# Gate first, then up in place, and a second Strassen level for one product of a gated feed-forward block

## The chip, the cores and the metric

The kernel runs on one core of one Trainium2 chip. The metric is the device time of one launch in microseconds (us); the profile's span, from the first to the last instruction, is 1.7 to 1.8 us shorter. A core has a matmul engine (TensorE, PE in the profile; its weight loads are a row of their own, PEld), VectorE (DVE), ScalarE (ACT), GpSimd (POOL) and a queue for transfers (SP). The kernel's matmuls read their operands from SBUF and write to PSUM, which the kernel uses as 8 banks of 512 fp32 columns. All runs told of here are with a granted TensorE clock of 0.999 or 1.000.

## The reference

A block of linear attention is followed by a gated feed-forward block (FFN), bf16, 2048 tokens, width 1024, hidden width F = 3584. Only the second half matters here:

```
h    = x + attention(layernorm(x))
n    = layernorm(h)
gate = n @ W_gate;  up = n @ W_up        # 1024 x 3584 each
gate = gate * (gate > 0)                 # ReLU
out  = h + (gate * up) @ W_down          # 3584 x 1024
```

## The kernel before

The tokens are taken in two passes of 1024. In each pass the gate and up products come first, then the down product. Products are done with Strassen's method (Winograd's form): 7 products of halved blocks stand in for 8, at the price of sums of the blocks before and of partial results after. The down product mostly uses two levels of it, gate and up one level.

One call of `strassen_pair` is a *unit*: two tiles of 128 columns of F, for gate (`w` = 0) and up (`w` = 1). `prod` is 4 matmuls of 512 columns into one PSUM bank. `S` are sums of token blocks, made once a pass; `T` are sums of weight blocks, made on VectorE one unit ahead (`fillin`). ScalarE forks a partial result to a second bank (`fk1`, `fk2`) so that two outputs can share it.

```python
BA, BE, BB, BC_ = [0, 1], [2, 3], [4, 5], [6, 7]          # PSUM banks
for w in range(2):
    prod(w, BA[w], w_blk(w, 0, 0), a_blk(0, 0), True, "P1")
    ident_act(bank(BB[w]), bank(BA[w]), ..., "fk1")
fillin(1)
for w in range(2):
    prod(w, BE[w], t_blk(w, 0), s_blk(0), True, "P5")      # the fifth product
    ident_act(ftmp[:, w, :], bank(BE[w]), ..., "s5")
# ... P6 into BB, fork to BC_; P2 into BA, evacuated
for w in range(2):
    prod(w, BB[w], t_blk(w, 2), s_blk(2), False, "P7")
    # ...
    add_s5(c22[:, w, :], bank(BB[w]), ..., w, ...)         # VectorE: bank + s5
relu(c22[:, 0, :], ...)
# ...
for w in range(2):
    prod(w, BC_[w], w_blk(w, 1, 1), s_blk(3), False, "P3")
    # ...
    add_s5(c12[:, w, :], bank(BC_[w]), ..., w, ...)
    if w == 0:
        mul(hh[...], c22[:, 0, :], c22[:, 1, :], ...)      # relu(gate) * up
# ... P4 into BB, evacuated
```

A planner records every operation with the buffers that it reads and writes and derives the semaphore waits from them; a PSUM bank is one buffer. Each engine runs its list in order. All matmuls are issued by one helper, so they share one line in the profile (L766) and are told apart by their operands: weights (stationary) in RWG or, summed, in RO; tokens in RH or, summed, in RC.

## Time and profile before

| | before |
|---|---|
| device time, median of 4 runs | 728.61 us (727.99 to 729.51) |
| span of the profiled run | 727.0 us |
| gate/up, first pass and second pass | 169.21 us each |
| one unit | 12.085 us |
| VectorE busy in the second pass | 116.3 of 169.2 us |

The stages come from the matmuls in order of time, at their seams. Columns: start, length of the merged row, engine, line, operation, operands, shapes, count.

```profile
230.48 1.89 PE L766 MATMUL ps<-RH,RWG 128*128 128x512 bf16 x8
...
399.69 5.34 PE L766 MATMUL ps<-RE,RAB 128*128 128x512 bf16 x24
...
475.91 1.69 PE L766 MATMUL ps<-RW,RAB 128*128 128x256 bf16 x14
...
646.65 5.34 PE L766 MATMUL ps<-RE,RAB 128*128 128x512 bf16 x24
```

The first row is the first product of the first pass; the second and fourth begin the down products, so 399.69 - 230.48 = 169.21 us is the first pass. The third row is the last product of the first down product: 14 x 109.2 ns after its start, at 477.44, the second pass begins (its first matmul has no record in this trace), and 646.65 - 477.44 is 169.21 again. Both are 14 x 56 matmuls at 215.8 ns.

### The profile page before, as it was taken

The numbers are of one execution on the slowest core, as the hardware profiler recorded it, in microseconds if no ns is written. First come the engines' busy times: TensorE is split into PE (matmuls) and PEld (weight loads), VectorE is DVE, ScalarE is ACT, GpSimd is POOL, SyncE is SP. The second block draws the span as 40 slices with busy tenths as digits, with TensorE's granted clock in tenths as the row PEclk, the third lists the DMA queues.
The fourth block names the chain that finished last, engine by engine and source line by source line (L and its number), as shares of the span: only waits on it lengthen the run. The fifth ranks groups of instructions, "written<-read, shape, count | busy, mean of one in ns | idle before, by whom it ended". The sixth has DMA issues, their size and how long they took to land.

```text
span 727.0 us, 11794 instructions
## 1 busy us (share of the span) xinstructions
PE 716.0 (98%) x4381; PEld 375.7 (52%) x4437; DVE 566.1 (78%) x978; ACT 363.9 (50%) x632; POOL 105.4 (15%) x177
## 2 busy tenths in 40 slices
PE   8999999999999999999999999999999999999998
PEld 3444444344444444444444668854444444447887
DVE  7878867798776988989888687866868675776884
ACT  4878666864841457686854311135454545433010
POOL 1411100000360103322311001310000000000331
PEclk9999999999999999999999999999999999999999
DMA  9642244024999897999999999994363572037996
GB/s 314 207 114 61 37 136 156 7 30 67 204 214 266 238 279 213 286 299 303 297 298 267 309 254 325 315 215 136 110 194 111 151 249 77 0 100 246 321 316 178
DMA packets 192985, 143.58 MB, mean 198 GB/s; under 512 B 51872, under 2 KB 170400, under 8 KB 192928
## 3 DMA queue, kind: packets, MB, share of 16 engines
q1 hardware_dynamic: 188224, 138.50, 65.9%
q0 software_dynamic: 4032, 3.67, 3.6%
q8 instruction: 35, 0.57, 0.3%
q10 hardware_dynamic: 672, 0.66, 0.3%
q14 instruction: 22, 0.18, 0.1%
HBM read 98.76 MB, written 32.51 MB: 181 GB/s over the span
## 4 chain that ended last, share of the span: by engine, by line
PE 89%; DVE 5%; ACT 2%; DMA 2%; issue 1%; POOL 0%; ACTq 0%; DVEq 0%; SPq 0%
PE ps L766 89%; DMA RE<-in_A_x_dram 1%; DVE RAB L852 1%; DVE RE L1227 1%; ACT RX L845 1%; DMA RE<-RE 1%; DVE RX L849 1%; ACT RXH L804 1%; ACT ps L771 0%; DVE st L780 0%; DVE RX L1068 0%; DVE rden L1225 0%; DVE RE L1532 0%; DVE RXH L1251 0%; DVE RXH L834 0%
## 5 line engine op out<-in xcount | busy, mean ns | idle before, releaser
L771 ACT ACTIVATE ps<-ps 128x512 f32<-128x512 f32 x178 | 103.6, 582 | 183.6 <-PE ps L766 181.1
L766 PE MATMUL ps<-RC,RO 128*128 128x512 f16 x672 | 154.2, 379 | 0.0
L766 PEld LDWEIGHTS ps<-RC,RO 128*128 128x128 f16 x672 | 65.8, 98 | 79.3
L766 PE MATMUL ps<-RH,RWG 128*128 128x512 bf16 x447 | 105.6, 379 | 0.1
L1409 DVE TENSOR_TENSOR RAB<-ps,RAB 128x512 bf16<-128x512 f32 x56 | 38.6, 689 | 65.4 <-PE ps L766 65.4
L766 PE MATMUL ps<-RC,RWG 128*128 128x512 f16 x320 | 76.9, 379 | 0.1
L1405 DVE TENSOR_TENSOR RE<-ps,RE 128x512 bf16<-128x512 f32 x112 | 74.4, 684 | 1.7 <-PE ps L766 0.7
L766 PEld LDWEIGHTS ps<-RH,RWG 128*128 128x128 bf16 x448 | 43.8, 98 | 52.6
L771 ACT ACTIVATE RE<-RE 128x512 bf16<-128x512 bf16 x56 | 35.1, 627 | 60.6 <-DVE RE L1405 59.9
L766 PE MATMUL ps<-RW,RE 128*128 128x512 bf16 x243 | 56.7, 379 | 1.9 <-DVE RXH L1251 0.7
L766 PE MATMUL ps<-RAB 128*128 128x512 bf16 (+2 forms) x266 | 56.6, 351 | 0.8 <-ACT RAB L912 0.5
L766 PE MATMUL ps<-RH,RO 128*128 128x512 bf16 (+1 forms) x228 | 55.3, 379 | 1.5
L1541 POOL DMA_DIRECT2D out_dram<-RX x20 | 17.9, 1261 | 266.0 <-DVE RX L1532 223.5
L771 ACT ACTIVATE RE<-ps 128x512 f32<-128x512 f32 x64 | 37.6, 598 | 32.1 <-PE ps L766 32.0
L766 PE MATMUL ps<-RW,RAB 128*128 128x256 f16 (+3 forms) x358 | 52.5, 300 | 0.2
L766 PEld LDWEIGHTS ps<-RC,RWG 128*128 128x128 bf16 (+1 forms) x320 | 30.0, 98 | 40.0 <-ACT ps L771 6.0
L1532 DVE TENSOR_TENSOR RE<-ps,RE 128x512 f32<-128x512 f32 x44 | 30.2, 686 | 17.7 <-PE ps L766 14.2
L766 PEld LDWEIGHTS ps<-RW,RAB 128*128 128x128 f16 (+1 forms) x362 | 35.4, 98 | 14.3
L771 ACT ACTIVATE RAB<-ps 128x512 bf16<-128x512 f32 x56 | 33.4, 597 | 16.1 <-PE ps L766 15.0
L1353 DVE TENSOR_TENSOR RO<-RWG 128x1024 f16<-128x1024 bf16 x54 | 36.9, 684 | 5.1 <-DMA RWG<-in_B_W_up_dram 5.1
L766 PEld LDWEIGHTS ps<-RH,RO 128*128 128x128 f16 (+1 forms) x256 | 24.4, 98 | 30.1 <-ACT RX L771 1.6
L766 PEld LDWEIGHTS ps<-RW,RE 128*128 128x128 bf16 x256 | 23.9, 98 | 29.3 <-DVE RXH L1251 1.2
(153 smaller groups left out, 1051.3 us busy)
## 6 DMA issues: line engine op xcount, KB each, us to landing
RWG<-in_B_W_gate_dram SPq DMA_DIRECT2D x28, 512.0 KB, 5.0
RWG<-in_B_W_up_dram SPq DMA_DIRECT2D x28, 512.0 KB, 6.3
RW<-l_scr SPq DMA_DIRECT2D x20, 448.0 KB, 6.3
RW<-in_B_W_down_dram SPq DMA_DIRECT2D x14, 512.0 KB, 5.5
t_scr<-RW SPq DMA_DIRECT2D x14, 512.0 KB, 4.6
l_scr<-RX SPq DMA_DIRECT2D x7, 1024.0 KB, 6.3
RE<-l_scr SPq DMA_DIRECT2D x15, 448.0 KB, 4.7
RE<-in_A_x_dram SPq DMA_DIRECT2D x23, 256.0 KB, 3.6
```

The source lines that it names most:

```text
L766: lambda e: e.matmul(out_ap, lhsT, rhs, start=start, stop=stop, skip_group_check=skip),
L771: PL.add("act", lambda e: e.activation(out=dst, in_=src, func=func), reads=reads, writes=writes, name=name)
L804: PL.add("act", lambda e: e.activation(out=junk[:, c0:c1], in_=src[:, c0:c1], func=func, scale=scale, accum_out=sv[:, col:col + 1]), reads ...
L845: PL.add("act", lambda e: e.activation(out=Et[:, k, :], in_=src, func=ACTF.Exp), reads=[src_buf], writes=[B_E[k]], name=name + "_exp")
L849: PL.add("dve", lambda e: e.tensor_scalar(out=Et[:, k, :], in0=Et[:, k, :], scalar1=1.0, scalar2=1e-6, op0=ALU.min, op1=ALU.add), reads=[] ...
L852: PL.add("dve", lambda e: e.scalar_tensor_tensor(out=dst_ap, in0=src, scalar=C1, in1=Et[:, k, :], op0=ALU.add, op1=ALU.max), reads=[src_bu ...
L1227: PL.add("dve", lambda e: e.tensor_tensor(out=osb[:, k, :].rearrange("p (g h e) -> p g h e", h=HPG, e=Dh), in0=nv[:, :, :, 0:Dh], in1=rden ...
L1353: PL.add(eng, lambda e: e.tensor_tensor(out=tb(j, u), in0=f0(u), in1=f1(u), op=ALU.subtract), reads=[B_w[i + x] for x in r] + ([B_T[k + x] ...
L1405: PL.add("dve", lambda e: e.tensor_tensor(out=dst, in0=src, in1=ftmp[:, w, :], op=ALU.add), reads=[bsrc, B_s5[w]], writes=[bdst], name=name)
L1409: PL.add("dve", lambda e: e.tensor_tensor(out=dst, in0=a_, in1=b_, op=ALU.mult), reads=reads, writes=[wr], name=name)
L1532: PL.add(eng, lambda e: e.tensor_tensor(out=dst, in0=in0, in1=in1, op=op), reads=reads, writes=writes, name=name)
L1541: PL.add("pool", lambda e: e.dma_start(dst, src, accum_op=ALU.add), reads=[bsrc], writes=[B_hscr[st]], slot=sl, name="acc_%d_%d" % (st, dh))
```

## The change

Its intent is to take matmul columns out of the fifth product by a second level of Strassen, where VectorE has room to make the extra sums: in the second pass. For a second level over the columns of weights as well, a unit has to hold two pairs of F tiles of the *same* matrix. So the order becomes: four tiles of gate, ReLU, stored in the hidden buffer; then the same four tiles of up, multiplied in place. The second level runs where `ps_ in L2F`, and `L2F = (1,)` is the second pass. The comments in the cut below are added.

```diff
-            q, which = (L // 2) % NPAIR, L % 2
+            n_ = (L // 2) % NPAIR
+            q, which = n_ - n_ % 2 + L % 2, n_ % 2        # which: 0 gate, 1 up
 ...
-        def strassen_pair(ps_, q, fill, mid):
+        def x_inner():                 # four sums of the summed tokens, once
+        def w_inner(n):                # three sums of summed weights, every unit
+        def ffn_unit(ps_, n, fill, mid):
+            up = n % 2
 ...
+            def evac(k, t, u, b, name):
+                d, db = H(k, t, u)
+                if up:                 # VectorE: multiply in place
+                    ... tensor_tensor(out=d, in0=bank(b), in1=d, op=ALU.mult) ...
+                else:                  # ScalarE: ReLU
+                    ident_act(d, bank(b), ..., func=ACTF.Relu)
 ...
+            if ps_ in L2F:             # sub: 2 matmuls of 256 columns
+                sub(cX, B_X, B_(0, 0), A(0, 0), True, "M1")
+                sub(cD, B_D, G(0), XS(0), False, "M5")
+                ident_act(c0, cX, ..., "M1c")
+                p1(0)
+                p1(1)
+                sub(cX, B_X, G(1), XS(1), False, "M6")
+                s5(1, 0, cX, B_X, "M6c")          # ScalarE copies cX
+                sub(c0, B_bank[BE[0]], B_(1, 0), A(0, 1), False, "M2")
+                fillin(2 if up else 3)
+                p2(0)
 ...
+                sub(cX, B_X, G(2), XS(2), False, "M7")
+                s5(1, 1, cX, B_X, "M7c")
+                s5_add(1)                         # VectorE adds cD
+                p6(0); p2(1); p6(1)
 ...
+                sub(cX, B_X, G(3), A(1, 1), False, "M4")
+                sub(cD, B_D, B_(1, 1), XS(3), False, "M3")
+                ...                               # copy, s5_add(0)
+            else:
+                ...                               # P1, P5, P6, P2 as before
```

`cX` and `cD` are the two halves of one bank; `c0` is half of another. The buffers `r11` and `r12`, which held ReLU results between gate and up, go.

More of the change, by code (lines that the diff above doesn't have):

```diff
@@ L243, in bass_sequential_preLN__linear_attn_block__glu_gated_reglu__prompt_kernel @@
         out2 = RAB[:, o0:o0 + 4 * SBW].rearrange("p (a b) -> p a b", a=STB)
-        r11 = RAB[:, o0:o0 + 2 * SBW].rearrange("p (a b) -> p a b", a=2)
-        o0 += 2 * SBW
-        r12 = RAB[:, o0:o0 + 2 * SBW].rearrange("p (a b) -> p a b", a=2)
         RC = sb("RC", [P, NDC * D], bf16)
@@ L282, in bass_sequential_preLN__linear_attn_block__glu_gated_reglu__prompt_kernel @@
         c12 = RE[:, 3 * D:4 * D].rearrange("p (a b) -> p a b", b=SBW)
+        xs5 = RE[:, 4 * D:6 * D].bitcast(f16).rearrange("p (j k t) -> p j k t", j=4, k=2)
+        g5 = RE[:, 6 * D:8 * D].bitcast(f16).rearrange("p (s j c) -> p s j c", s=2, j=4)
         hnE = RE[:, 4 * D:8 * D].rearrange("p (t a c) -> p t a c", t=STB, c=P)
@@ L439, in bass_sequential_preLN__linear_attn_block__glu_gated_reglu__prompt_kernel @@
         B_U, B_V = B_f[0:4], B_f[4:8]
-        B_r11 = bufs("r11_", 2)
-        B_r12 = bufs("r12_", 2)
+        B_g5 = [bufs("g5_%d_" % i, 4) for i in range(2)]
+        B_s5q = [bufs("s5q%d_" % i, 2) for i in range(2)]
+        B_xs5 = bufs("xs5_", 4)
         B_out2 = bufs("out2_", STB)
@@ L518, in bass_sequential_preLN__linear_attn_block__glu_gated_reglu__prompt_kernel @@
             b_.over = B_hnE
-        for b_ in flat(B_hh) + B_r11 + B_r12:
+        for b_ in flat(B_hh) + B_out2:
             b_.over = flat(B_xnT) + flat(B_pqT)
@@ L1370, in hh_sums, with A, X, add @@
                    reads=[B_hh[f1][0]], writes=[B_hh[f1][1]], name="D3_%d" % q)
-        def strassen_pair(ps_, q, fill, mid):
-            Lg = (ps_ * NPAIR + q) * 2
-            f1, f2 = 2 * q, 2 * q + 1
-            L = [Lg, Lg + 1]
-            iw = [l % NWG for l in L]
-            kt = [l % NTR for l in L]
-            BA, BE, BB, BC_ = [0, 1], [2, 3], [4, 5], [6, 7]
-            rr = q % 2
-            def fillin(n):
-                for _ in range(n):
+        def x_inner():
+            def A(t, k):
+                return Ssum[:, 0, 2 * k:2 * k + 2, t * SHB:(t + 1) * SHB], [B_S[0]]
+            def X(j):
+                return xs5[:, j], [B_xs5[j]]
+            def add(j, x, y, op):
+                PL.add("dve", lambda e: e.tensor_tensor(out=xs5[:, j], in0=x[0], in1=y[0], op=op), reads=x[1] + y[1],
+                       writes=[B_xs5[j]], name="xs%d" % (j + 1))
+            return [lambda: add(0, A(1, 0), A(1, 1), ALU.add), lambda: add(1, X(0), A(0, 0), ALU.subtract),
+                    lambda: add(2, A(0, 0), A(1, 0), ALU.subtract), lambda: add(3, A(0, 1), X(1), ALU.subtract)]
@@ new lines, in w_inner, with T, add @@
+        def w_inner(n):
+            z = n % 2
+            k = (2 * n) % NTR
+            bt = [B_T[k][0], B_T[k + 1][0]]
+            def T(kh, u):
+                return Tring[:, k + u, 0, 2 * kh:2 * kh + 2, :].rearrange("p a c -> p (a c)")
+            def add(dst, a_, b_, rd, wr):
+                PL.add("dve", lambda e: e.tensor_tensor(out=dst, in0=a_, in1=b_, op=ALU.subtract), reads=bt + rd,
+                       writes=wr, name="g5_%d" % n)
+            g = B_g5[z]
+            o2 = 2 * P
+            t01 = Tring[:, k:k + 2, 0, 0:2, :].rearrange("p s a c -> p s (a c)")
+            t1 = Tring[:, k + 1, 0, :, :].rearrange("p (s a) c -> p s (a c)", s=2)
+            return [lambda: add(g5[:, z, 0:4:2, :], t1, t01, [], [g[0], g[2]]),
+                    lambda: add(g5[:, z, 1, :], T(1, 1), g5[:, z, 0, :], [g[0]], [g[1]]),
+                    lambda: add(g5[:, z, 3, :], T(1, 0), g5[:, z, 1, :], [g[1]], [g[3]])]
@@ new lines, in bass_sequential_preLN__linear_attn_block__glu_gated_reglu__prompt_kernel, with H, H2, fillin @@
+        later = []
+        def ffn_unit(ps_, n, fill, mid):
+            Lg = (ps_ * NPAIR + n) * 2
+            up = n % 2
+            iw = [(Lg + u) % NWG for u in range(2)]
+            kt = [(Lg + u) % NTR for u in range(2)]
+            f0 = 2 * (n - up)
+            BA, BE, BB, BC_ = [0, 1], [2, 3], [4, 5], [6, 7]
+            if ps_ in L2F:
+                BE, BB = BB, BE
+            if up:
+                BB, BC_ = BC_, BB
+            z = n % 2
+            fl = (1, 1) if ps_ not in L2F or n == NPAIR - 1 else (1, 0) if up else (2, 1)
+            def H(k, t, u):
+                return hh[:, f0 + 2 * u + k, t * SBW:(t + 1) * SBW], B_hh[f0 + 2 * u + k][t]
+            def H2(k, t):
+                return hh[:, f0 + k:f0 + k + 3:2, t * SBW:(t + 1) * SBW], [B_hh[f0 + k][t], B_hh[f0 + 2 + k][t]]
+            def fillin(n_):
+                for _ in range(n_):
@@ L1383, in fillin, with go @@
                     if fill:
                         fill.pop(0)()
+            def go(fs):
+                for f_ in fs:
+                    f_()
             def a_blk(k, t):
@@ L1390, in s_blk, with w_blk, t_blk, prod @@
                 return (lambda kk: Ssum[:, i, kk, :]), [B_S[i]]
-            def w_blk(w, k, h):
-                return (lambda kk: wring[:, iw[w], k * KH + kk, h * P:(h + 1) * P]), [B_w[iw[w]]]
-            def t_blk(w, j):
-                return (lambda kk: Tring[:, kt[w], j, kk, :]), [B_T[kt[w]][j]]
-            def prod(w, b, st_, mov, start, name):
+            def w_blk(u, k, h):
+                return (lambda kk: wring[:, iw[u], k * KH + kk, h * P:(h + 1) * P]), [B_w[iw[u]]]
+            def t_blk(u, j):
+                return (lambda kk: Tring[:, kt[u], j, kk, :]), [B_T[kt[u]][j]]
+            def prod(u, b, st_, mov, start, name):
                 (sf, sr), (mf, mr) = st_, mov
@@ L1401, in prod @@
                     mm(bank(b), sf(kk), mf(kk), start and kk == 0, kk == KH - 1, sr + mr, B_bank[b],
-                       "%s%s_%d_%d" % (name, "gu"[w], ps_, q), skip=True)
-            def add_s5(dst, src, bsrc, w, bdst, name):
-                PL.add("dve", lambda e: e.tensor_tensor(out=dst, in0=src, in1=ftmp[:, w, :], op=ALU.add),
-                       reads=[bsrc, B_s5[w]], writes=[bdst], name=name)
-            def mul(dst, a_, b_, reads, wr, name):
-                PL.add("dve", lambda e: e.tensor_tensor(out=dst, in0=a_, in1=b_, op=ALU.mult), reads=reads,
-                       writes=[wr], name=name)
@@ L1412, in relu @@
-            def relu(dst, src, reads, wr, name):
-                ident_act(dst, src, reads, [wr], name, func=ACTF.Relu)
-            for w in range(2):
-                prod(w, BA[w], w_blk(w, 0, 0), a_blk(0, 0), True, "P1")
-                ident_act(bank(BB[w]), bank(BA[w]), [B_bank[BA[w]]], [B_bank[BB[w]]], "fk1")
-            fillin(1)
-            for w in range(2):
-                prod(w, BE[w], t_blk(w, 0), s_blk(0), True, "P5")
-                ident_act(ftmp[:, w, :], bank(BE[w]), [B_bank[BE[w]]], [B_s5[w]], "s5")
@@ L1422, in strassen_pair @@
-            fillin(1)
-            for w in range(2):
-                prod(w, BB[w], t_blk(w, 1), s_blk(1), False, "P6")
-                ident_act(bank(BC_[w]), bank(BB[w]), [B_bank[BB[w]]], [B_bank[BC_[w]]], "fk2")
-            fillin(1)
-            for f_ in mid[0]:
-                f_()
-            for w in range(2):
-                prod(w, BA[w], w_blk(w, 1, 0), a_blk(1, 0), False, "P2")
-                if w == 0:
-                    relu(r11[:, rr, :], bank(BA[0]), [B_bank[BA[0]]], B_r11[rr], "rl11")
-                    for f_ in mid[2]:
-                        f_()
@@ L1435, in strassen_pair @@
-            mul(hh[:, f1, 0:SBW], bank(BA[1]), r11[:, rr, :], [B_bank[BA[1]], B_r11[rr]], B_hh[f1][0], "hh11")
-            fillin(1)
-            for w in range(2):
-                prod(w, BB[w], t_blk(w, 2), s_blk(2), False, "P7")
-                run(mid[4], 1)
-                add_s5(c22[:, w, :], bank(BB[w]), B_bank[BB[w]], w, B_c22[w], "c22")
-            relu(c22[:, 0, :], c22[:, 0, :], [], B_c22[0], "rl22")
-            for f_ in mid[3]:
-                f_()
-            for w in range(2):
-                prod(w, BC_[w], w_blk(w, 1, 1), s_blk(3), False, "P3")
-                run(mid[4], 1)
-                add_s5(c12[:, w, :], bank(BC_[w]), B_bank[BC_[w]], w, B_c12[w], "c12")
-                if w == 0:
-                    mul(hh[:, f2, SBW:2 * SBW], c22[:, 0, :], c22[:, 1, :], B_c22, B_hh[f2][1], "hh22")
@@ L1450, in strassen_pair @@
-            relu(c12[:, 0, :], c12[:, 0, :], [], B_c12[0], "rl12")
-            for f_ in mid[1]:
-                f_()
-            for w in range(2):
-                prod(w, BB[w], t_blk(w, 3), a_blk(1, 1), False, "P4")
-                if w == 0:
-                    relu(r12[:, rr, :], bank(BB[0]), [B_bank[BB[0]]], B_r12[rr], "rl21")
-            mul(hh[:, f2, 0:SBW], c12[:, 0, :], c12[:, 1, :], B_c12, B_hh[f2][0], "hh12")
-            mul(hh[:, f1, SBW:2 * SBW], bank(BB[1]), r12[:, rr, :], [B_bank[BB[1]], B_r12[rr]], B_hh[f1][1], "hh21")
@@ L1459, in strassen_pair, with evac5, fin5 @@
-            if ps_ > 0 or q < NPAIR - 2:
+                       "%s%s_%d_%d" % (name, "gu"[up], ps_, n), skip=True)
+            def evac5(k, t, u, src, bsrc, tmp, btmp, name):
+                d, db = (tmp[:, u, :], btmp[u]) if up else H(k, t, u)
+                PL.add("dve", lambda e: e.tensor_tensor(out=d, in0=src, in1=ftmp[:, u, :], op=ALU.add),
+                       reads=[bsrc, B_s5[u]], writes=[db], name=name)
+            def fin5(k, t, tmp, btmp, name):
+                d, db = H2(k, t)
+                if up:
+                    PL.add("dve", lambda e: e.tensor_tensor(out=d, in0=d, in1=tmp, op=ALU.mult), reads=btmp, writes=db,
+                           name=name)
+                else:
+                    PL.add("act", lambda e: e.activation(out=d, in_=d, func=ACTF.Relu), reads=[], writes=db, name=name)
@@ new lines, in evac, with p1 @@
+            def evac(k, t, u, b, name):
+                d, db = H(k, t, u)
+                if up:
+                    PL.add("dve", lambda e: e.tensor_tensor(out=d, in0=bank(b), in1=d, op=ALU.mult),
+                           reads=[B_bank[b]], writes=[db], name=name)
+                else:
+                    ident_act(d, bank(b), [B_bank[b]], [db], name, func=ACTF.Relu)
+            def p1(u):
+                prod(u, BA[u], w_blk(u, 0, 0), a_blk(0, 0), True, "P1")
+                ident_act(bank(BB[u]), bank(BA[u]), [B_bank[BA[u]]], [B_bank[BB[u]]], "fk1")
@@ new lines, in p6, with p2, sub, B_ @@
+            def p6(u):
+                prod(u, BB[u], t_blk(u, 1), s_blk(1), False, "P6")
+                ident_act(bank(BC_[u]), bank(BB[u]), [B_bank[BB[u]]], [B_bank[BC_[u]]], "fk2")
+            def p2(u):
+                prod(u, BA[u], w_blk(u, 1, 0), a_blk(1, 0), False, "P2")
+                evac(0, 0, u, BA[u], "h11")
+            if ps_ in L2F:
+                cX, cD, c0 = ps[:, BE[1], 0:SHB], ps[:, BE[1], SHB:2 * SHB], ps[:, BE[0], 0:SHB]
+                B_X = B_D = B_bank[BE[1]]
+                tb = [B_T[kt[0]][0], B_T[kt[1]][0]]
+                def sub(dst, bdst, w, x, start, name):
+                    for kk in range(2):
+                        mm(dst, w[0](kk), x[0](kk), start and kk == 0, kk == 1, w[1] + x[1], bdst,
+                           "%s_%d_%d" % (name, ps_, n), skip=True)
+                def B_(kh, u):
+                    return (lambda kk: Tring[:, kt[u], 0, 2 * kh + kk, :]), [tb[u]]
+                def G(j):
+                    return (lambda kk: g5[:, z, j, kk * P:(kk + 1) * P]), [B_g5[z][j]]
+                def A(t, k):
+                    return (lambda kk: Ssum[:, 0, 2 * k + kk, t * SHB:(t + 1) * SHB]), [B_S[0]]
+                def XS(j):
+                    return (lambda kk: xs5[:, j, kk, :]), [B_xs5[j]]
+                def s5(u, t, src, b, name):
+                    ident_act(ftmp[:, u, t * SHB:(t + 1) * SHB], src, [], [b, B_s5q[u][t]], name)
+                def s5_add(t):
+                    d = ftmp[:, 1, t * SHB:(t + 1) * SHB]
+                    PL.add("dve", lambda e: e.tensor_tensor(out=d, in0=cD, in1=d, op=ALU.add), reads=[],
+                           writes=[B_D, B_s5q[1][t]], name="s5a%d" % t)
+                for u in range(2):
+                    for t in range(2):
+                        B_s5q[u][t].over = [B_s5[u]]
+                sub(cX, B_X, B_(0, 0), A(0, 0), True, "M1")
+                sub(cD, B_D, G(0), XS(0), False, "M5")
+                ident_act(c0, cX, [], [B_X, B_bank[BE[0]]], "M1c")
+                p1(0)
[5 more added lines that the diff above has]
+                p2(0)
+                go(mid[2])
+                sub(cX, B_X, G(2), XS(2), False, "M7")
+                s5(1, 1, cX, B_X, "M7c")
+                s5_add(1)
+                p6(0)
+                p2(1)
+                p6(1)
+                go(mid[0])
+                sub(cX, B_X, G(3), A(1, 1), False, "M4")
+                sub(cD, B_D, B_(1, 1), XS(3), False, "M3")
+                e_ = ps[:, BE[0]:BE[0] + 2, 0:SHB]
+                PL.add("act", lambda e: e.activation(out=ftmp[:, 0, :].rearrange("p (t c) -> p t c", t=2), in_=e_,
+                                                     func=ACTF.Identity), reads=[B_bank[BE[0]]],
+                       writes=[B_X, B_s5[0]], name="M4c")
+                go(later)
+                later.clear()
+                fillin(2 if up else 3)
+                s5_add(0)
+                B_s5[1].over = B_s5q[1]
+                B_s5[1].w = B_s5q[1][0].w
+            else:
+                p1(0)
+                p1(1)
+                fillin(1)
+                for u in range(2):
+                    prod(u, BE[u], t_blk(u, 0), s_blk(0), True, "P5")
+                    ident_act(ftmp[:, u, :], bank(BE[u]), [B_bank[BE[u]]], [B_s5[u]], "s5")
+                fillin(1)
+                p6(0)
+                p6(1)
+                go(later)
+                later.clear()
+                fillin(1)
+                go(mid[0])
+                p2(0)
+                go(mid[2])
+                p2(1)
+                fillin(1)
@@ new lines, in ffn_unit @@
+            for u in range(2):
+                prod(u, BB[u], t_blk(u, 2), s_blk(2), False, "P7")
+                run(mid[4], 1)
+                evac5(1, 1, u, bank(BB[u]), B_bank[BB[u]], c22, B_c22, "c22")
+            fin5(1, 1, c22, B_c22, "h22")
+            go(mid[3])
+            fillin(fl[0])
+            for u in range(2):
+                prod(u, BC_[u], w_blk(u, 1, 1), s_blk(3), False, "P3")
+                run(mid[4], 1)
+                evac5(1, 0, u, bank(BC_[u]), B_bank[BC_[u]], c12, B_c12, "c12")
@@ L1460, in strassen_pair @@
+            if up:
+                fin5(1, 0, c12, B_c12, "h12")
+            else:
+                later.append(lambda: fin5(1, 0, c12, B_c12, "h12"))
+            go(mid[1])
+            fillin(fl[1])
+            for u in range(2):
+                prod(u, BB[u], t_blk(u, 3), a_blk(1, 1), False, "P4")
+                evac(0, 1, u, BB[u], "h21")
+            if ps_ > 0 or n < NPAIR - 2:
                 load_w_next()
@@ L1736, in down_pass @@
             claim(B_sgo, flat(B_T))
-            claim(B_out2, B_r11 + B_r12)
             sg6 = l2_sums(q_d2, sgs[1], "sg6")
@@ L1779, in down_pass @@
             claim(B_c12, [U[1][3]])
-            claim(B_r11 + B_r12, B_out2)
         load_x1(0, split=True)
@@ L1968, in bass_sequential_preLN__linear_attn_block__glu_gated_reglu__prompt_kernel @@
         wl_q = []
+        L2F = (1,)
         ln_q = []
@@ L1975, in bass_sequential_preLN__linear_attn_block__glu_gated_reglu__prompt_kernel @@
                 if q + 1 < NPAIR:
-                    fill = fill + t_sums((p_ * NPAIR + q + 1) * 2)
-                if q > 0:
-                    hh_sums(q - 1)
+                    t_ = t_sums((p_ * NPAIR + q + 1) * 2)
+                    if p_ in L2F:
+                        t_ = t_[0:1] + w_inner(q + 1) + t_[1:]
+                    fill = fill + t_
                 mid = [[], [], [], [], []]
+                if q > 0 and q % 2 == 0:
+                    mid[0].append(lambda q=q: hh_sums(q - 2))
+                    mid[3].append(lambda q=q: hh_sums(q - 1))
                 if p_ == 0:
@@ L2017, in bass_sequential_preLN__linear_attn_block__glu_gated_reglu__prompt_kernel @@
                         mid[1] += g_[2:4]
-                strassen_pair(p_, q, fill, mid)
+                ffn_unit(p_, q, fill, mid)
                 if p_ == 1 and q == NM + 1:
@@ L2031, in bass_sequential_preLN__linear_attn_block__glu_gated_reglu__prompt_kernel @@
             assert not fill
+            hh_sums(NPAIR - 2)
             hh_sums(NPAIR - 1)
+            if p_ in L2F:
+                claim(B_V, B_xs5 + flat(B_g5))
             late = []
@@ L2047, in bass_sequential_preLN__linear_attn_block__glu_gated_reglu__prompt_kernel, with claim_xs @@
                 late += [(nxt_t, (5, 0))] + [(ts[i], (6, i)) for i in range(4)]
+                if p_ + 1 in L2F:
+                    def claim_xs():
+                        claim(B_xs5, B_V)
+                        claim(flat(B_g5), B_V)
+                    gi = w_inner(0)
+                    xi = x_inner()
+                    late += [(claim_xs, (6, 0)), (xi[0], (6, 3)), (xi[1], (6, 4)), (xi[2], (6, 4)), (xi[3], (6, 5))]
+                    late += [(gi[0], (6, 4)), (gi[1], (6, 5)), (gi[2], (6, 5))]
                 def nxt_w():
```

## The prediction

> **What bounds the kernel now.** I read the busy shares first, then the chain of work that ended last, then that chain in order of time, then the matmuls of one stage in order of time, and last the busy time of each engine by stage. From the page:
>
> ```profile
> PE 716.0 (98%) x4381; PEld 375.7 (52%) x4437; DVE 566.1 (78%) x978; ACT 363.9 (50%) x632; POOL 105.4 (15%) x177
> ...
> PE 89%; DVE 5%; ACT 2%; DMA 2%; issue 1%; POOL 0%; ACTq 0%; DVEq 0%; SPq 0%
> ```
>
> TensorE is busy 98% of the span and makes up 89% of the chain, but busy time of pipelined matmuls proves little, so I look at their pitch. The chain in order of time shows the gate/up product of the second token pass as equal pieces:
>
> ```profile
> 500.10 12.03 PE ps L766 x55
> 512.19 12.03 PE ps L766 x55
> 524.28 12.03 PE ps L766 x55
> ```
>
> Pieces start 12.09 us apart, and the source has 14 products of 4 matmuls, 56, in each unit: 12.085 / 56 = 215.8 ns for a matmul of 512 columns. No gap is left over: 28 units (14 in each token pass), 338 us in all, are bound by TensorE and by nothing else. The matmuls in order of time, first of such a unit, then of the down product, where two-level Strassen is already used:
>
> ```profile
> 503.34 3.62 PE L766 MATMUL ps<-RC,RO 128*128 128x512 f16 x16
> 506.79 1.89 PE L766 MATMUL ps<-RH,RWG 128*128 128x512 bf16 x8
> ...
> 658.74 1.69 PE L766 MATMUL ps<-RW,RC 128*128 128x256 f16 x14
> 660.27 1.69 PE L766 MATMUL ps<-RW,RO 128*128 128x256 f16 x14
> ```
>
> The x16 are the fifth and sixth products of gate and up; the next row starts 3.45 us later, 16 x 215.8 ns. In the down product 14 matmuls of 256 columns start 1.53 us before the next 14: 109.2 ns each, although each needs its own weight load. So a matmul of half the width costs 0.506 of a full one here, and splitting products is nearly free for TensorE.
>
> How much room the other engines have, per two units (first row: first token pass; second: second pass):
>
> ```profile
> core 0: us, PE busy (x) PEld busy (x) DVE busy (x) ACT busy (x) POOL busy (x), PEclk, DMA share, GB/s
> 300.00:324.20 24.20, 24.09 (x112) 11.00 (x113) 21.31 (x41) 18.15 (x31) 6.75 (x13) 1.00 1.00 282
> 512.19:536.36 24.17, 24.07 (x110) 10.95 (x112) 17.64 (x37) 11.95 (x21) 0.00 (x0) 1.00 0.55 153
> ```
>
> VectorE is 88% busy in the first pass and 73% in the second; ScalarE 75% and 49%. The added work falls in the second pass, where there is room. The granted clock is 1.00.
>
> **What the Trainium skill says.** "TensorE: Matmul & The Clock Gate", section "Wait — 56ns, not 53.3ns?", puts warm back-to-back matmuls at N / 2.4 GHz + about 2.5 ns: 215.8 ns at 512 columns and 109.2 ns at 256. The trace agrees to the tenth. The same page, section "Step-by-step: what each phase is for", says the next weights load while a matmul runs; the trace agrees (98 ns loads under a 109 ns pitch). "Perfetto Trace Analysis", section "Optimizing Scalar/DVE Operations", says grouping into larger operations saves overhead; here a VectorE multiply of 512 bf16 elements takes 418 ns and an add of 1024 takes 686 ns, so merging two saves about 0.15 us. "PSUM — Partial Sum Buffer", section "Terms", says TensorE must not write a bank while ScalarE or VectorE accesses it; the new code orders its work by whole banks accordingly, which is where new waits can arise. No run yet shows a collision.
>
> **The change, part by part.** (1) The order of work. A unit was two F tiles of gate and of up; it becomes four F tiles of gate alone, then of up alone, multiplied in place over the stored gate. Products per unit, matmuls, weight bytes and the fork copies stay. TensorE: 0. ScalarE's and VectorE's evacuations also stay in number, but are uneven: ReLU evacuations go to the gate unit, the multiplies from PSUM (689 ns) to the up unit. Four SBUF multiplies of 418 ns become two of 1024 elements at about 686 ns: -0.3 us of VectorE per two units.
>
> (2) The fifth product in the second pass. Removed per unit: 8 matmuls of 512 columns, 8 x 215.8 = 1.726 us. Added: seven sub-products of 2 matmuls of 256 columns, 14 x 109.2 = 1.529 us. Saved 0.198 us a unit, all of it on the path; 14 units give **2.77 us**. A unit should go from 12.085 to 11.89 us. Nothing is saved in the first pass.
>
> (3) VectorE pays for it, per unit: three sums of weights (one of 512 elements, about 0.42 us, two of 256, 0.28 us each: 0.99) and two adds from half a bank. A full-bank add takes 684 ns; taking 512 columns at 0.96 GHz as 533 ns, half a bank is about 0.42 us (estimate), so 0.84. Two units: 17.64 + 2 x 1.83 - 0.3 = 21.0 of 23.8 us, 88%: as full as VectorE is in the first pass without holding TensorE up. Once only: four sums of the tokens, about 0.42 us each.
>
> (4) ScalarE, per unit: the two s5 copies (598 ns each) become one of two half banks (about 0.6 us) and three of half a bank. From 192 columns at 318 ns and 512 at 597 ns, 256 columns take about 0.37 us (estimate): +0.5 us. Not a bound.
>
> (5) New waits inside a unit. I lay TensorE out at the pitches above: M1 and M5 end at 0.44 us, the two first products at 1.30 and 2.16, M6 at 2.38, M2 at 2.60, P2 at 3.46, then M7. From the timeline, ScalarE starts some 0.26 us after a product's last slot, and a dependent matmul starts 0.05 us after its release. The **tightest place is M7**, which overwrites the accumulator that ScalarE must first have copied: the second fork copy starts at 2.42 and takes 0.58, to 3.00; the copy of M6 follows, to 3.37; M7 is due at 3.46. It fits with 0.1 us to spare. The next, M4, is due at 6.27 and waits for VectorE's half-bank add at about 5.1: 1.1 us. The last product P4 is due at 10.2 and needs its bank evacuated by about 9: 1.2 us. If every unit missed M7 by 0.05 us, that would be 0.7 us over 14.
>
> (6) Start and end. The token sums and the first weight sums are squeezed into the last part of the first down product. VectorE idled there 0.6 to 0.8 us twice in the run before; I find them done about half a microsecond before M5 needs them, so between 0 and 0.5 us of stall. At the end of each pass two sums of the hidden tiles instead of one trail into the down product, 0.9 us more of VectorE: its first quarter runs 12.1 us of matmuls that don't need them, so this is hidden.
>
> Sum: 728.8 - 2.8 + 0.5 for small waits (M7, the start, and semaphore waits between short pairs of matmuls) = **726.5 us**.
>
> **Rivals.** (a) VectorE becomes the bound of the second pass. For: in the units that also sum down weights its record time reaches 96% if I add bare durations; the queue is in order, so one late add delays all behind it. Against: records overlap (independent adds of 684 ns start 0.60 us apart in its timeline), the union in the first pass is 88% without a TensorE gap, and the real sum is 21.0 of 23.8. If it were the bound, each of six or seven late units would lose 0.3 us or more: near 728.5.
> (b) The unevenness hurts the first pass: up units there need some 13 us of VectorE, gate units about 10, against 12.085 each. For: every slack in (5) shrinks by the backlog of 2 to 3 us. Against: the backlog meets no TensorE wait before the next unit's gate evacuations, which ScalarE now does; two units together still fit. If wrong, up to 14 x 0.3 = 4 us lost: 730.
> (c) Short pairs of matmuls with waits between do not reach 109.2 ns. For: the down product has 14 in a row with one wait, here only two. Against: dependencies are mostly satisfied long before. At 123 ns each the whole saving would be gone: 728.8.
> (d) The 3 us gap of TensorE near 686 us, where VectorE is late in the last down product, could swallow the gain. Against: VectorE idled 2.2 us waiting for TensorE at 672 us, so it isn't still working off the FFN there; the gap moves earlier with everything else.
>
> **Range and chances.** All saved and nothing lost is 726.0, and I know of no further saving; the run-to-run spread is 1 us. Below 725.3 is unlikely. Losing the whole gain (c, or a mild a) gives 728.8; 729.2 as upper end leaves one in ten for (b). Two per cent is 14.6 us: the saving cannot reach it, and a loss that size would need a stall of 0.5 us in every one of the 28 units. Faster 0.01, same 0.97, slower 0.02.
>
> **What would show it.** The chain by time must show units of the second pass 11.89 us apart and those of the first still 12.085. The 256-column matmuls of the fifth product should start 109 ns apart; gaps ahead of M7 or M4 would confirm (5). VectorE in two units of the second pass should be busy near 21 of 23.8 us. A unit in either pass longer than these, with TensorE waiting on VectorE, would prove (a) or (b). The prediction is wrong if first-pass units stretch, or if the second pass starts with a gap over 1 us.

## The result, and the profile after

The changed kernel took 725.64 us (725.28 to 726.18, 4 runs) against 728.61 for the kernel before: a ratio of 0.9959, 95% interval 0.9942 to 0.9976. The ratios come from all fast runs of both kernels, so they are not quite the ratio of the medians. The time lies within the predicted range, 0.9 us under the predicted value, and by the 2% measure the two are the same.

The page, busy shares and chain:

```profile
PE 717.1 (99%) x4521; PEld 384.6 (53%) x4521; DVE 587.2 (81%) x1024; ACT 361.0 (50%) x632; POOL 109.5 (15%) x177
...
PE 89%; DVE 6%; ACT 2%; issue 1%; SPq 1%; DMA 1%; POOL 0%; DVEq 0%; ACTq 0%
```

These shares have hardly moved, and TensorE's busy time even rose while the kernel got faster; its records overlap (379 ns each at a pitch of 215.8), and the trace of before lacks some of them: 4381 matmuls against 4437 weight loads, where the changed kernel has 4521 of both. The seams tell more:

```profile
229.75 1.89 PE L767 MATMUL ps<-RH,RWG 128*128 128x512 bf16 x8
...
398.96 5.34 PE L767 MATMUL ps<-RE,RAB 128*128 128x512 bf16 x24
...
476.76 0.38 PE L767 MATMUL ps<-RC,RO 128*128 128x256 f16 x2
...
643.20 5.34 PE L767 MATMUL ps<-RE,RAB 128*128 128x512 bf16 x24
```

First pass: 398.96 - 229.75 = 169.21 us, as before. Second pass: 643.20 - 476.76 = **166.44 us, 2.77 us less**. The rest of this trace's difference, 0.73 us, lies ahead of the first row, in code that the change does not touch. One unit of the second pass, again in order of time:

```profile
500.54 0.38 PE L767 MATMUL ps<-RC,RO 128*128 128x256 f16 x2
500.75 0.38 PE L767 MATMUL ps<-RE 128*128 128x256 f16 x2
500.97 1.89 PE L767 MATMUL ps<-RH,RWG 128*128 128x512 bf16 x8
502.70 0.38 PE L767 MATMUL ps<-RE 128*128 128x256 f16 x2
502.92 0.38 PE L767 MATMUL ps<-RC,RO 128*128 128x256 f16 x2
503.14 1.03 PE L767 MATMUL ps<-RH,RWG 128*128 128x512 bf16 x4
504.00 0.38 PE L767 MATMUL ps<-RE 128*128 128x256 f16 x2
```

The rows are M1, M5, the first products, M6, M2, P2 and M7. A pair of short matmuls takes 0.22 us from start to start, 109 ns each, with no "idle before" on any row. The unit before starts at 488.65, so a unit is 11.89 us; all starts of units in this pass lie 11.88 or 11.89 us apart. ScalarE in the same stretch shows the place that the prediction called tightest (columns as above, then the idle time before and its releaser):

```profile
502.10 0.58 ACT L772 ACTIVATE ps<-ps 128x512 f32<-128x512 f32 x1 [0.50 <-PE ps L767]
502.96 0.58 ACT L772 ACTIVATE ps<-ps 128x512 f32<-128x512 f32 x1 [0.28 <-PE ps L767]
503.45 0.38 ACT L772 ACTIVATE RE<-ps 128x256 f32<-128x256 f32 x1
```

These are the two forks and the copy of M6. The copy ends at 503.45 + 0.38 = 503.83 and M7 starts at 504.00: 0.17 us to spare. VectorE over two units, first pass and second (columns as in the prediction's table by stage):

```profile
300.00:324.20 24.20, 24.20 (x114) 10.98 (x112) 21.70 (x39) 17.77 (x29) 7.55 (x13) 1.00 1.03 279
505.60:529.40 23.80, 23.80 (x126) 12.13 (x125) 20.57 (x45) 11.96 (x23) 0.00 (x0) 1.00 0.56 156
```

It is busy 20.57 of 23.80 us in the second pass, and over the whole second pass 134.1 us where it was 116.3.

### The profile page after: what moved, and what is told of

The parts are those of the page before. It is cut to its first block, busy times and chain, and to the rows that moved or that the text cites. A ratio compares the mean times of both kernels' runs of the same rounds, so it can differ in the third digit from the quotient of the medians.

```text
span 723.5 us, 12104 instructions
## 1 busy us (share of the span) xinstructions
PE 717.1 (99%) x4521; PEld 384.6 (53%) x4521; DVE 587.2 (81%) x1024; ACT 361.0 (50%) x632; POOL 109.5 (15%) x177
## 4 chain that ended last, share of the span: by engine, by line
PE 89%; DVE 6%; ACT 2%; issue 1%; SPq 1%; DMA 1%; POOL 0%; DVEq 0%; ACTq 0%
PE ps L767 89%; SPq L565 1%; DVE RAB L853 1%; DMA RE<-in_A_x_dram 1%; DVE RE L1228 1%; DVE RX L850 1%; ACT RX L846 1%; DVE RX L1069 1%; ACT RXH L805 1%; DVE RW L963 0%; DVE RWG L988 0%; ACT ps L772 0%; DVE RE L853 0%; DVE rden L1226 0%; DVE RE L1661 0%
## 5 line engine op out<-in xcount | busy, mean ns | idle before, releaser
L772 ACT ACTIVATE ps<-ps 128x512 f32<-128x512 f32 (+1 forms) x192 | 108.8, 567 | 218.0 <-PE ps L767 210.8
L767 PE MATMUL ps<-RC,RO 128*128 128x512 f16 x616 | 143.0, 369 | 0.0
L767 PE MATMUL ps<-RH,RWG 128*128 128x512 bf16 x448 | 108.1, 379 | 0.0
L767 PEld LDWEIGHTS ps<-RC,RO 128*128 128x128 f16 x616 | 60.3, 98 | 63.5
L767 PE MATMUL ps<-RH,RO 128*128 128x512 bf16 (+1 forms) x256 | 61.2, 379 | 0.0
L772 ACT ACTIVATE RE<-ps 128x512 f32<-128x512 f32 (+1 forms) x64 | 31.5, 503 | 37.8 <-PE ps L767 37.8
L1456 DVE TENSOR_TENSOR RAB<-ps,RE 128x512 bf16<-128x512 f32 x56 | 37.1, 685 | 2.8 <-PE ps L767 1.9
L1465 ACT ACTIVATE RAB<-RAB 128x1024 bf16<-128x1024 bf16 x28 | 29.5, 1055 | 19.4 <-DVE RAB L1456 18.9
```

Of the source, the lines that this page charges most:

```text
L767: lambda e: e.matmul(out_ap, lhsT, rhs, start=start, stop=stop, skip_group_check=skip),
L772: PL.add("act", lambda e: e.activation(out=dst, in_=src, func=func), reads=reads, writes=writes, name=name)
L1456: PL.add("dve", lambda e: e.tensor_tensor(out=d, in0=src, in1=ftmp[:, u, :], op=ALU.add), reads=[bsrc, B_s5[u]], writes=[db], name=name)
L1465: PL.add("act", lambda e: e.activation(out=d, in_=d, func=ACTF.Relu), reads=[], writes=db, name=name)
```

## The experiments

**Theory:** TensorE alone sets the time of both gate/up passes; the gain is the columns removed, the 2.77 us of the prediction's part (2), and nothing else. **Rivals:** the new order of work itself gives or costs time; VectorE is in truth close to its bound; ScalarE's copy ahead of M7 is not the tightest place. All stages below are read at the seams shown above. "Rest" runs from the start of the second down product to the end of the span.

| run | gate/up starts at | first pass | down | second pass | rest | median us |
|---|---|---|---|---|---|---|
| before | 230.48 | 169.21 | 77.75 | 169.21 | 80.35 | 728.61 |
| changed | 229.75 | 169.21 | 77.80 | 166.44 | 80.30 | 725.64 |
| order alone | 230.23 | 169.22 | 77.75 | 169.21 | 80.29 | 729.02 |
| changed, again | 230.45 | 169.21 | 77.80 | 166.43 | 80.31 | 725.75 |
| half depth | 230.85 | 169.62 | 77.79 | 157.36 | 80.28 | 716.67 |
| M6 copied twice | 230.22 | 169.21 | 77.80 | 170.83 | 80.34 | 730.08 |
| VectorE +2, second pass | 230.99 | 169.21 | 77.80 | 166.82 | 80.38 | 726.62 |
| VectorE +1, first pass | 230.15 | 169.22 | 77.79 | 166.44 | 80.30 | 725.56 |
| VectorE +3, first pass | 230.19 | 178.02 | 77.79 | 166.44 | 80.36 | 734.46 |

The kernel before had a median of 728.43 us beside the order alone, the repeat, half depth and M6 twice, and 728.79 beside the three with more VectorE work.

### The order alone

```diff
-        L2F = (1,)
+        L2F = ()
```

> The new order of work alone (gate for four tiles, then up in place), with the fifth product left as it was. If the whole gain comes from the matmul columns removed from the fifth product, this equals the kernel before: 728.6 us within 0.5, and units of 12.085 us in both passes. If the order itself helps (the rest of the measured 3.0 us beyond the 2.77 worked out, or more), it comes out 0.3 us or more below before; if the unevenness of VectorE's work costs something that the second level hid, it is above before.

729.02 us (5 runs), ratio to before 1.0006, interval 0.9993 to 1.0018: no difference that these runs can show. Both passes keep 169.2 us. The order neither gives nor costs; it only makes the second level possible.

### The changed kernel again

> The changed kernel once more, unaltered, beside the order alone on the same chip. If the second level is worth what its columns say, this is 2.77 us (0.4%) below the order alone and, if the order is worth nothing, 2.77 us below before: near 725.8. The first units of the gate and up product should start within 1 us of the kernel before; the 0.7 us by which they started earlier in the first profile would be chance of the loads ahead of it, and should not come back at the same size.

725.75 us (5 runs), ratio to before 0.996, interval 0.9946 to 0.9973. Against the order alone on the same chip it is 3.3 us faster by the medians, of which the second pass accounts for 169.21 - 166.43 = 2.78. Gate/up starts at 230.45 here, 0.03 us from before; over all nine traces it starts between 229.75 and 230.99, whatever the kernel. So the 0.73 us by which the first trace was ahead there was chance.

### Half depth

```diff
-                    for kk in range(2):
-                        mm(dst, w[0](kk), x[0](kk), start and kk == 0, kk == 1, ...
+                    for kk in range(1):
+                        mm(dst, w[0](kk), x[0](kk), start and kk == 0, True, ...
```

> Wrong result on purpose: each of the seven sub-products has one matmul in place of two. If TensorE alone bounds the second pass, 14 units lose 7 x 109.2 ns each, 10.7 us in all: 714.9 us. But the sub-products also give ScalarE time: with them halved, the copy of M6 is done about 0.17 us after M7 is due, by the working of the prediction, so I expect units of 11.12 + 0.17 = 11.3 us and about 717 us. If VectorE (20.6 of 23.8 us busy) is in truth near its bound, the units stay above 11.5 us and the time above 720.

716.67 us, and 157.36 us in the second pass, 11.24 us a unit: near the 11.3 us expected with the wait for M6's copy, and above the 11.12 without any. The trace shows the wait:

```profile
514.14 1.03 PE L767 MATMUL ps<-RH,RWG 128*128 128x512 bf16 x4
515.11 0.28 PE L767 MATMUL ps<-RE 128*128 128x256 f16 x1
```

Four matmuls of 215.8 ns from 514.14 end at 515.00; M7 starts at 515.11, 0.11 us late, and 11.12 + 0.11 = 11.23. VectorE, with the same work in shorter units, did not hold them up: with the work that it has, VectorE is not near its bound. (The profiled run is the slowest of the four, 717.67 us. Its first pass is 0.4 us longer, because P4 of the first unit starts 0.39 us late: the view shows 0.23 us idle there, waiting for VectorE. The same code shows no such wait in the two traces of the unaltered changed kernel; why it came here is not known.) One warning: this kernel computes the fifth product wrongly and still passed the comparison with the reference. Its tolerance does not see an error of this size in the FFN, so passing says little about this part. That the second level is right I checked only by writing out its sums from the source.

### M6 copied twice

```diff
                 s5(1, 0, cX, B_X, "M6c")
+                s5(1, 0, cX, B_X, "M6c")
```

> ScalarE copies M6 twice (same result). The trace has 0.17 us between the end of that copy and the start of M7. If this is the tightest place, one more copy of 0.38 us makes M7 late by 0.38 - 0.17 = 0.2 us, plus some 0.06 if the second waits for the first: 14 x 0.2 to 0.26 = 2.9 to 3.7 us lost, so 728.6 to 729.3, the whole gain. If there is more room there than I think, the time stays at 725.7.

730.08 us, 4.3 us more than the changed kernel by the medians; the second pass grew by 4.39 us, 0.31 us a unit. I expected 0.2 to 0.26. The timeline of ScalarE and then of TensorE:

```profile
516.75 0.79 ACT L772 ACTIVATE RE<-ps 128x256 f32<-128x256 f32 x2
```

```profile
516.43 1.03 PE L767 MATMUL ps<-RH,RWG 128*128 128x512 bf16 x4
517.60 0.39 PE L767 MATMUL ps<-RE 128*128 128x256 f16 x2
```

The two copies end at 516.75 + 0.79 = 517.54, M7 follows 0.06 us later, and it was due at 516.43 + 4 x 0.2158 = 517.29: 0.31 us late. My 0.17 us of room had left out these 0.06 us from a copy's end to the matmul that it releases; the true room is about 0.11. The place is confirmed as the tightest, and 0.4 us of ScalarE in the wrong spot costs more than the whole change gains: the ratio to the kernel before is 1.0022, interval 1.0008 to 1.0036.

### More work for VectorE

```diff
                     t_ = t_sums((p_ * NPAIR + q + 1) * 2)
+                    if p_ == 1:                                        # or 0
+                        t_[2] = lambda f_=t_[2]: [f_() for _ in range(3)]   # or 2, or 4
```

The third sum of weights is simply made again, with the same result: two repeats in the second pass, one in the first, three in the first.

> In the second pass VectorE does one of its sums of weights three times in place of once (same result): about 2 x 0.7 us more in each of 13 units, 2.8 us more per two units. It is busy 20.6 of 23.8 us now in the early units and some 2.3 us less in the late ones, so by the sum it still fits, at 98% in the early ones: if sums are what counts, the time moves by less than 0.5 us. If VectorE is nearer to its bound than its busy time says, since its queue is in order and waits in places, each of the early units grows by 0.3 us or more and the time by over 2 us.

726.62 us, and 0.38 us more in the second pass. The medians moved by more than the 0.5 us expected, 0.9 us from the changed kernel's repeat, but the rest is not in this pass: in the profiled run gate/up starts 0.5 us later. VectorE is now busy 22.80 of 23.80 us in the same stretch. The view flags no idle time of TensorE, but the starts of the matmuls show the 0.38 us: ten of the thirteen distances between units are 11.88 or 11.89 us, three are 12.01 to 12.02. In one of these three, ScalarE and then TensorE:

```profile
515.72 1.18 ACT L772 ACTIVATE ps<-ps 128x512 f32<-128x512 f32 x2 [0.98 <-DVE RAB L1456]
```

```profile
516.05 0.38 PE L767 MATMUL ps<-RC,RO 128*128 128x256 f16 x2
516.36 1.04 PE L767 MATMUL ps<-RH,RWG 128*128 128x512 bf16 x4
```

The first fork waited for VectorE to empty its bank, and P2, which writes into the bank that this fork reads, starts at 516.36 where 516.05 + 2 x 0.1092 = 516.27 was due. So VectorE does reach TensorE's path here, by way of ScalarE's forks. The busy time grew by 2.2 us per two units and nearly all of it fitted, as the sum said.

> The same in the first pass, one repeat: 0.7 us more of VectorE a unit, 1.4 per two units on top of 21.7 of 24.2. If the uneven load of gate and up units is harmless there, as the prediction argues, it fits and the time stays within 0.5 us of 725.7. If the unevenness had used up the slack, the first pass grows by 0.1 us a unit or more, 1.4 us or more in all.

725.56 us, the first pass 169.22. VectorE is busy 22.98 of 24.20 us there, 1.3 us more. The uneven load of gate and up units costs nothing.

> Three repeats in the first pass: about 2.1 us more of VectorE a unit, about what the second level of the fifth product costs VectorE in the second pass (1.83). 21.7 + 4.2 = 25.9 of 24.2 us per two units: over the bound. I expect the first pass to grow by at least 0.85 us a unit in most of its units, 8 to 12 us in all, which is more than the 2.77 us that the second level could save there. If it grows by under 2.77 us, the second level could pay in the first pass too.

734.46 us; the first pass grew by 8.81 us, at the low end of what was expected. TensorE now waits once in every two units, always ahead of P4, whose bank VectorE has not yet emptied:

```profile
317.89 1.90 PE L767 MATMUL ps<-RH,RO 128*128 128x512 bf16 x8 [1.31 <-DVE RAB L1456]
343.55 1.90 PE L767 MATMUL ps<-RH,RO 128*128 128x512 bf16 x8 [1.31 <-DVE RAB L1456]
```

Two units take 343.55 - 317.89 = 25.66 us where they took 24.17. The repeats put as much on VectorE as the second level did in the second pass: there 20.57 us of busy time against 17.18 with the order alone, 3.4 us per two units; here it is busy 25.08 of these 25.66 us, again 3.4 more than the 21.7 before. So the first pass could hardly carry the second level in every unit, which is an estimate from these sums: 21.7 + 3.4 = 25.1 us of VectorE against two units of 23.8. A second level in the first pass, in all or in some of its units, was not run. Whether it would pay in some stays open, and no version that beats the changed kernel came of these runs.

## Why the prediction was right or wrong

- **What bounds the kernel: right.** From the start of gate/up on, every stage but the second gate/up pass kept its length to 0.1 us, and this one followed the count of its matmul columns. With half the sub-product matmuls taken out as well, it shrank by another 9.1 us, until ScalarE's copy held it.
- **The order of work (1): right.** Zero for TensorE; the order alone measured a ratio of 1.0006, with 1 inside its interval.
- **The fifth product (2): right to the hundredth.** 2.77 us worked out, 2.77 and 2.78 in two traces; units of 11.89 us.
- **VectorE's bill (3): right in kind, a little high.** 21.0 us per two units expected, 20.57 measured. The adds from half a bank took 425 ns (0.42 estimated) and the small sums 423 and 290 ns. Their records overlap (two adds of 684 ns took 1.28 us together), so a sum of bare durations overstates it: the second level added 3.4 us where 2 x 1.83 was expected, and the order alone took off 0.46 (17.64 to 17.18) where 0.3 was.
- **ScalarE (4): right.** 0.37 us was estimated for 256 columns; 372 ns into PSUM and 380 ns into SBUF were measured.
- **The new waits (5): right place; the size of the slack was right by luck.** "It fits with 0.1 us to spare": no wait occurred, and the runs put the room at 0.11 us. But the prediction's sum, 3.46 - 3.37, leaves out the 0.05 us after a release that it names itself, so by its own terms only 0.04 us were left. It also lets the copy of M6 begin when the second fork ends; in the trace the copy begins at 503.45, 0.09 us before the fork's record ends at 502.96 + 0.58 = 503.54. The two errors nearly cancel.
- **Start and end (6), and the sum: too cautious.** The prediction set aside 0.5 us for "small waits". There were none in either trace of the changed kernel: its gate/up passes are 169.21 and 166.43 to 166.44 us, the bare matmul sums. The remaining 0.4 us between 726.0 and the measured 725.64 is within what the untouched part ahead of gate/up varies by, 1.2 us over nine traces; 0.2 of it is the base, 728.8 before the fourth run of the kernel before.
- **Rivals (a) to (c): they fell.** VectorE stayed off the path with 1.3 us more per two units in the first pass, cost 0.4 us in all with 2.2 more in the second, and bound the first pass with 3.4 more (all as measured busy time); pairs of short matmuls kept 109 ns.
- **Rival (d): rightly rejected, but its premise was a misreading.** There is no "3 us gap of TensorE near 686 us". I took the stretch in which the chain runs through VectorE for idle time of TensorE. The matmuls of the kernel before show otherwise:

```profile
683.19 6.28 PE L766 MATMUL ps<-RW,RAB 128*128 128x256 f16 x56
689.54 1.70 PE L766 MATMUL ps<-RWG,RAB 128*128 128x256 f16 x14
```

56 matmuls at 109.2 ns from 683.19 last to 689.31, so the gap is 0.2 us. The chain followed VectorE for 3 us back from that short wait, while TensorE worked beside it.

## What to carry to other kernels

Where a stage runs at the bare pitch of its matmuls, count columns: what a change takes away comes off the time in full, as long as the order of the other engines' work leaves every bank free in time. Lay out one unit slot by slot beforehand and find the place with the least room; here 0.11 us on ScalarE decided between a gain and a loss, while 1.3 us more of VectorE per two units went unnoticed in the first pass and 2.2 us more cost 0.4 us over the whole second pass. And read gaps from the engine's own timeline, since the chain's path through another engine is not idle time of the first.

## What the Trainium skill lacked or had wrong

- "ScalarE: Activation LUTs", section "What ACT_TABLE_LOAD costs", gives 186 ns plus 0.833 ns an element for an instruction with immediate scale and bias, and does not say from which memory. That makes, as an estimate, 0.40 us for 256 elements and 0.61 us for 512. From PSUM the runs show a little less, 0.37 to 0.38 and 0.58 to 0.60 us; a ReLU of 512 elements from SBUF took 0.63 us in the kernel before.
- "Perfetto Trace Analysis", section "Optimizing Scalar/DVE Operations", puts VectorE's overhead on PSUM at about 125 ns. With 512 columns at the 0.96 GHz of "VectorE: DVE Perf Modes", section "Specifications", that makes, as an estimate, 658 ns an add. Two independent adds from PSUM took 1.28 us together at 684 ns each, so they start 0.60 us apart, an overhead of some 65 ns.
- No page that I read gives the hand-over times on which the tightest place rested: 0.10 us from the modelled end of a matmul's record to the start of the ScalarE operation that it releases (500.97 + 1.89 = 502.86 to 502.96; the record itself outlasts the slot by 0.16 us, which makes the 0.26 us of the prediction), and 0.06 us from the end of a copy to the matmul that it releases (517.54 to 517.60).
